# Moving two memsets to VectorE ahead of the input, list-scheduling the last head's chain, and port intervals in the schedule's model

## The chip, the cores and the metric

The kernel runs on one core of a Trainium2 chip. The metric is device time in microseconds (us), the median over several executions. The profile covers one execution and shows its span, which is 1.7 to 2.5 us shorter than the time of the same execution in all runs here (696.9 against 698.68 for the profiled run of the kernel before; 704.4 against 706.56 after). Ratios below are the mean time of one kernel's fast runs over that of the other's of the same rounds, so not quite the ratio of the medians that are quoted. A run counts as fast when its time is within 1.5% of the fastest of the same kernel. Rounds differ: the kernel before has a median of 697.48 to 698.98 in them, so differences between kernels of different rounds are good to about 1.5 us.

Names: PE is TensorE, PEld its weight load, DVE is VectorE, ACT is ScalarE, POOL is GpSimd, SP is SyncE, whose queue issues most transfers. "ps" is PSUM, the matmul output memory; "PV" is the product of the probabilities with V.

## The reference

```python
def reference(A_x, A_wqkv, A_wo, B_x, B_w1, B_b1, B_w2, B_b2):
    x = A_x                                  # 1 x 2048 x 512, bf16
    xn = _layernorm(x)
    # A: softmax attention, 32 heads of 16, over 2048 tokens, then @ wo
    # B: layernorm again, token-mixing MLP 2048 -> 1376 -> 2048 with gelu
    return x + _A_ref(xn, A_wqkv, A_wo) + _B_ref(xn, B_w1, B_b1, B_w2, B_b2)
```

Attention is the bulk: 32 heads x 2048 x 2048 exponentials. The kernel works them off as 1024 tiles of 128 x 1024.

## The kernel before

The kernel is Python code that orders every instruction itself. A model (`Sched`) keeps a time at which each engine comes free; the part up to the end of "block 0" (the first 16 periods of two tiles) is written in fixed order, and the rest comes from a greedy loop that takes at each step what the model says can start first. Each engine's order of instructions is then fixed.

```python
def port_time(self, eng, t):                       # the model's port of VectorE and GpSimd:
    return max(t, self.port_free["pool" if eng == "dve" else "dve"])

def load_lib(lib):                                 # GpSimd's loadable library, with INT64_ADD
    sc.add("pool", lambda e: e.load_library(lib), cost=(LIB_I, LIB_I), name="lib", port=False)

def late_consts():
    load_lib(INT64_LIB)
    sc.add("pool", lambda e: e.memset(wo_t[:], 0.0), ...)
    ...                                            # loads of wo, one small cast (b1col) on GpSimd

# head: layer norm of the first four tiles of x
ln_sums(1); warm_up(N_WARM, 5); ln_stats(0); ...; ln_stats(3)
sc.add("pool", lambda e: e.memset(v17_main[:, :, 16:17], 1.0), ...)   # V's column of ones
for t in range(NPRE):
    ln_norm(t)
late_memsets()                                     # VM, on GpSimd

VM_AT = (2, 8, 12, 15)                             # VM = 13/16 of V, scaled on GpSimd
for period in range(NKT):                          # NKT = 16: block 0
    ...
    block0_work(period)
    if period in VM_AT:
        j = VM_AT.index(period)
        vm_scale(list(range(4 * j, 4 * j + 4)), 0) # a tensor_scalar on GpSimd
    if period == 13:
        ln2_stats()
late_consts()                                      # behind all of it
...                                                # the greedy loop, then tail()
```

An exponential is either one ACTIVATE on ScalarE, or a TENSOR_SCALAR on VectorE with three shifted copies, of which about two go to GpSimd as INT64_ADD. The latter needs four PV products in place of one.

The softmax here doesn't subtract the row's maximum and nothing guards it: scores larger than these inputs give would overflow.

## Time and profile before

| | us |
|---|---|
| time, median of 3 runs | 696.94 (696.93 to 698.19) |
| span of the profiled run | 696.9 |
| first exponential on ScalarE starts | 15.27 |
| last exponential on ScalarE ends | 685.03 |
| first instruction of the last head's chain on VectorE | 688.99 |

A timeline row has start, length, engine, source line, operation, output and input, and in brackets the idle time just ahead with what ended it; "issue" there means that the engine waited for nothing that the profile shows.

### The profile page before, as it was taken

Reading aid. Unit: us, or ns where it says so; the run is one execution under the profiler, and the core shown is the slowest. Engines: PE = TensorE matmul, PEld = TensorE weight load, DVE = VectorE, ACT = ScalarE, POOL = GpSimd, SP = SyncE. Lnnn points to the kernel's source line nnn. Section 1 sums busy time; section 2 is a strip of 40 time slices with the busy share of each in tenths; the row PEclk is TensorE's granted clock in tenths of the full one; section 3 lists DMA queues with packets and bytes.
Section 4 is the critical chain, followed back from the end, with each engine's and each line's share of the span. In section 5 each row is a group of like instructions: output and inputs, shape, how many; then the busy total and the mean of one; then the engine's idle time right before and its main releaser. Section 6 shows DMA issues by size and latency. Waiting matters only on the chain.

```text
span 696.9 us, 29358 instructions
## 1 busy us (share of the span) xinstructions
PE 678.8 (97%) x12916; PEld 312.0 (45%) x12916; DVE 621.3 (89%) x894; ACT 673.2 (97%) x736; POOL 402.2 (58%) x683
## 2 busy tenths in 40 slices
PE   7999999999999999999999999999999999999997
PEld 4433545445544444444444444444444444444443
DVE  7968998998989999989999999898998888888987
ACT  4999999999999999999999999999999999999993
POOL 4544556665356755756666576665766665654642
PEclk9999999999999999999999999999999999999999
DMA  7104200031102200022220212222220222213101
GB/s 211 33 4 82 54 22 20 19 72 28 25 13 52 47 23 19 19 55 46 50 39 22 48 38 54 53 56 53 52 60 20 54 54 57 70 35 81 45 23 44
DMA packets 85728, 32.32 MB, mean 46 GB/s; under 512 B 67424, under 2 KB 85600, under 8 KB 85600
## 3 DMA queue, kind: packets, MB, share of 16 engines
q1 hardware_dynamic: 85168, 30.05, 18.6%
q8 instruction: 101, 1.65, 1.0%
q10 hardware_dynamic: 432, 0.39, 0.2%
q14 instruction: 27, 0.22, 0.1%
HBM read 21.76 MB, written 2.35 MB: 35 GB/s over the span
## 4 chain that ended last, share of the span: by engine, by line
PE 80%; ACT 12%; DVE 4%; DMA 2%; issue 1%; POOL 0%; SPq 0%; DVEq 0%
PE ps L808 32%; PE ps L741 29%; PE ps L839 15%; ACT pT L765 8%; ACT x_sb L765 3%; PE ps L893 2%; DMA denb<-rden_scratch 1%; DVE pT L776 1%; DVE OT L1012 1%; ACT gT_sb L950 1%; DVE hx L549 0%; SPq L431 0%; DMA x_sb<-in_A_x_dram 0%; PE ps L590 0%; DVE oT L1048 0%
## 5 line engine op out<-in xcount | busy, mean ns | idle before, releaser
L765 ACT ACTIVATE pT<-ps 128x1024 bf16<-128x1024 f32 x535 | 523.2, 1132 | 3.3 <-PE ps L741 2.7
L776 DVE TENSOR_SCALAR pT<-ps 128x1024 int16<-128x1024 f32 x221 | 270.1, 1222 | 26.8 <-PE ps L741 20.8
L741 PE MATMUL ps<-QT,KT 32*128 32x512 bf16 x2048 | 284.8, 385 | 5.3 <-ACT pT L765 3.5
L782 POOL INT64_ADD pT<-pT x299 | 181.6, 616 | 129.5 <-DVE pT L785 74.2
L808 PE MATMUL ps<-pT,V 128*32 128x256 bf16 x4716 | 243.8, 276 | 2.9 <-DVE OT L1012 2.5
L765 ACT ACTIVATE x_sb<-ps 128x1024 bf16<-128x1024 f32 x182 | 197.9, 1141 | 0.2 <-PE ps L741 0.2
L741 PEld LDWEIGHTS ps<-QT,KT 32*128 32x128 bf16 x2048 | 78.8, 91 | 183.5 <-ACT pT L765 76.3
L808 PEld LDWEIGHTS ps<-pT,V 128*32 128x32 bf16 x4716 | 107.9, 96 | 85.8 <-issue 66.8
L782 POOL INT64_ADD x_sb<-pT x146 | 89.3, 616 | 57.0 <-DVE pT L785 32.7
L776 DVE TENSOR_SCALAR x_sb<-ps 128x1024 int16<-128x1024 f32 x86 | 105.1, 1222 | 14.7 <-PE ps L741 11.8
L808 PE MATMUL ps<-x_sb,V 128*32 128x256 bf16 x1836 | 116.7, 275 | 1.0 <-DVE OT L1012 0.6
L782 POOL INT64_ADD pT<-x_sb x132 | 79.9, 614 | 48.2 <-DVE pT L785 32.6
L785 DVE TENSOR_SCALAR pT<-pT 128x1024 int16<-128x1024 int16 x154 | 65.1, 426 | 4.5
L808 PE MATMUL ps<-pT,VM 128*32 128x256 bf16 x880 | 61.3, 275 | 0.5 <-DVE pT L785 0.5
L839 PE MATMUL ps<-gT_sb,wblk 128*32 128x512 bf16 (+1 forms) x704 | 61.2, 383 | 0.0
L808 PEld LDWEIGHTS ps<-x_sb,V 128*32 128x32 bf16 x1836 | 46.2, 96 | 31.0 <-issue 23.5
L839 PE MATMUL ps<-hx,wblk 128*32 128x512 bf16 x594 | 52.4, 383 | 0.0
L782 POOL INT64_ADD x_sb<-x_sb x47 | 28.6, 614 | 23.8 <-DVE pT L785 8.0
L847 PE MATMUL ps<-hx,wblk 32*128 32x512 bf16 (+1 forms) x96 | 37.1, 387 | 0.0
L785 DVE TENSOR_SCALAR x_sb<-pT 128x1024 int16<-128x1024 int16 x64 | 27.1, 428 | 1.8
L808 PEld LDWEIGHTS ps<-pT,VM 128*32 128x32 bf16 x880 | 23.3, 96 | 10.6 <-issue 8.8
L785 DVE TENSOR_SCALAR pT<-x_sb 128x1024 int16<-128x1024 int16 x58 | 24.5, 423 | 1.6
(113 smaller groups left out, 460.4 us busy)
## 6 DMA issues: line engine op xcount, KB each, us to landing
wblk<-in_B_w_dram SPq DMA_DIRECT2D x10, 512.0 KB, 4.4
wblk<-in_B_w_dram SPq DMA_DIRECT2D x16, 320.0 KB, 3.6
oC<-OT SPq DMA_DIRECT2D x248, 16.0 KB, 1.8
denb<-rden_scratch SPq DMA_DIRECT2D x124, 32.0 KB, 2.3
xr<-in_A_x_dram SPq DMA_DIRECT2D x16, 128.0 KB, 2.6
dcomp<-OT SPq DMA_DIRECT2D x124, 2.0 KB, 1.7
QT<-Qall SPq DMA_DIRECT2D x120, 16.0 KB, 1.8
out_dram<-osb SPq DMA_DIRECT2D x14, 128.0 KB, 2.0
```

Of the source, the lines that this page charges most:

```text
L741: specs.append(dict(eng="pe", fn=lambda e, r=r, bk=bk: e.matmul(bank(bk), lhsT=KT[32 * r:32 * r + 32, T, 128 * kt:128 * (kt + 1)], rhs=QT[ ...
L765: return [dict(eng="act", fn=lambda e: e.activation(buf(pbuf[n]), ps[:, s_ * 1024:(s_ + 1) * 1024], ACTF.Exp, scale=LN2_128), reads=[("ban ...
L776: return dict(eng="dve", fn=lambda e: e.tensor_scalar(buf_i(w), ps[:, s_ * 1024:(s_ + 1) * 1024], IBIAS, 0.0, ALU.add, ALU.max), reads=[(" ...
L782: return dict(eng=eng, fn=lambda e: e.int64_add(buf_i(o).bitcast(I64), buf_i(w).bitcast(I64), SHIFTS[k] * 0x0001000100010001), reads=[("pT ...
L785: return dict(eng=eng, fn=lambda e: e.tensor_scalar(buf_i(o), buf_i(w), float(SHIFTS[k]), 1.0, ALU.add, ALU.mult), reads=[("pT", w)], writ ...
L808: specs.append(dict(eng="pe", fn=lambda e, c=c, h=h, i=i, off=off: e.matmul(bank(PV_BANK)[32 * c:32 * c + 32, 256 * par:256 * par + 256], ...
L839: specs.append(dict(eng="pe", fn=lambda e, c=c, w=w: e.matmul(bank(EX_BANK)[32 * c:32 * c + w, :], lhsT=lhs_of(32 * c, 32 * c + w), rhs=rh ...
L847: return [dict(eng="pe", fn=lambda e: e.matmul(bank(EX_BANK)[0:dst_rows, :], lhsT=lhs_of(0, dst_rows)[rs], rhs=rhs[rs], start=begin, stop= ...
L893: return [dict(eng="pe", fn=lambda e, ct=ct, c=c: e.matmul(bank(EX_BANK)[32 * c:32 * c + 32, 128 * i:128 * (i + 1)], lhsT=xnT[:, ct, 128 * ...
L950: yield "act", [dict(eng="act", fn=lambda e, ap=ap: e.activation(ap, ap, ACTF.Gelu_apprx_tanh), reads=[("gT", f) for f in fts], writes=[(" ...
L1012: yield "pvev", [dict(eng="dve", fn=lambda e: e.tensor_copy(OT32[:, eb, :], bank(PV_BANK)), reads=[("bank", PV_BANK)], writes=[("OT32", eb)])]
```

## The change

The intent: (1) take V's ones and wo_t's zeros off GpSimd and put them on VectorE, which is idle until x arrives, so that the fourth layer norm no longer waits for GpSimd's memset; (2) let the last head's VectorE chain take its place by readiness, keep VectorE from taking the last two exponentials (D_END), and take the block's o_in transfers out of the way of its denominators; (3) model the shared port as intervals. In passing, the library load and the constants move from behind block 0 to its period 12 (LN2_AT). PER_LIST changes nothing at its value.

```diff
-D_LAST = 31
+PER_LIST = 16
+LN2_AT = 12
+D_END = 1022
...
-    def port_time(self, eng, t):
-        return max(t, self.port_free["pool" if eng == "dve" else "dve"])
+    def port_time(self, eng, t, dur):
+        for a, z in self.port_iv["pool" if eng == "dve" else "dve"]:
+            if t < z and t + dur > a:
+                t = z
+        return t
...
         def late_consts():
             load_lib(INT64_LIB)
-            sc.add("pool", lambda e: e.memset(wo_t[:], 0.0), ...)
...
+        late_memsets()
+        sc.add("dve", lambda e: e.memset(v17_main[:, :, 16:17], 1.0), ...)
+        sc.add("dve", lambda e: e.memset(wo_t[:], 0.0), ...)
         ln_sums(1)
...
+        ln_norm(0)
         ln_stats(3)
-        sc.add("pool", lambda e: e.memset(v17_main[:, :, 16:17], 1.0), ...)
-        for t in range(NPRE):
+        for t in range(1, NPRE):
             ln_norm(t)
-        late_memsets()
...
-            if period == 13:
+            if period == LN2_AT:
                 ln2_stats()
-
-        late_consts()
+                late_consts()
...
+        # task_o_in and task_last: generators for the greedy loop;
+        # the code of task_last stood at the start of tail() before
-                    if n % BN > D_LAST or ...:        # never true
+                    if n >= D_END:
                         continue
```

More of the change, by code (lines that the diff above doesn't have):

```diff
@@ L139, in __init__ @@
         self.pe_log = []
-        self.port_free = {"dve": 0.0, "pool": 0.0}
+        self.port_iv = {"dve": [], "pool": []}
         self.port_op = None
@@ L180, in _time @@
         if port:
-            ready = self.port_time(eng, max(self.free[eng], ready))
+            ready = self.port_time(eng, max(self.free[eng], ready), cost[0])
         if op.is_dma:
@@ L208, in _time @@
         if port:
-            self.port_free[eng] = op.t0 + cost[0]
+            self.port_iv[eng] = self.port_iv[eng][-7:] + [(op.t0, op.t0 + cost[0])]
     def pe_activity(self, t):
@@ L498, in late_consts @@
             load_lib(INT64_LIB)
-            sc.add("pool", lambda e: e.memset(wo_t[:], 0.0), writes=[("wo_t", z) for z in range(4)], cost=(1.75, 1.8))
             for e_ in range(2):
@@ L650, in bass_parallel_sum__softmax_full_mha__mixer_token_mlp__prompt_kernel @@
                writes=[("rcomp", 0)], cost=(1.4, 1.5))
+        late_memsets()
+        sc.add("dve", lambda e: e.memset(v17_main[:, :, 16:17], 1.0), writes=[("Vone",)], cost=(0.6, 0.65))
+        sc.add("dve", lambda e: e.memset(wo_t[:], 0.0), writes=[("wo_t", z) for z in range(4)], cost=(1.1, 1.15))
         ln_sums(1)
@@ L657, in bass_parallel_sum__softmax_full_mha__mixer_token_mlp__prompt_kernel @@
         ln_rstd(1, 2)
+        ln_norm(0)
         ln_stats(3)
-        sc.add("pool", lambda e: e.memset(v17_main[:, :, 16:17], 1.0), writes=[("Vone",)], cost=(2.28, 2.33))
-        for t in range(NPRE):
+        for t in range(1, NPRE):
             ln_norm(t)
-        late_memsets()
         TB = (0, 1, 2, 3)
@@ L705, in block0_work @@
                 warm_up(5, PV_BANK, KT[:, 0, 0:512], [("KTt", 0, z) for z in range(4)])
-            if period >= NKT - 2:
+            if NKT - 2 <= period < PER_LIST:
                 warm_up(3, 4, KT[:, 0, 0:512], [("KTt", 0, z) for z in range(4)])
@@ L1005, in bass_parallel_sum__softmax_full_mha__mixer_token_mlp__prompt_kernel, with task_o_in @@
         ot_free = set()
+        def task_o_in(b):
+            p, e_ = divmod(b, 2)
+            eb, tb_ = b % 2, p % 2
+            yield "gate", lambda: p < 2 or PAIRS[p - 2] in oT_done
+            for c in range(4):
+                h, i = divmod(c, 2)
+                for a in range(2):
+                    ro = 64 * e_ + 32 * a + 16 * i
+                    yield "sp", [dict(dst=oC32[ro:ro + 16, tb_, 256 * h:256 * h + 256],
+                                      src=OT32[32 * c:32 * c + 16, eb, 256 * a:256 * a + 256],
+                                      reads=[("OT32", eb)], writes=[("oC32", tb_, e_, c, a)], name="o_in")]
+            yield "call", lambda: ot_free.add(b)
         def task_epilogue(b):
@@ L1017, in task_epilogue @@
                                   reads=[("OT32", eb)], writes=[("dcomp", eb, c)], name="den_in")]
-            yield "gate", lambda: p < 2 or PAIRS[p - 2] in oT_done
-            for c in range(4):
-                h, i = divmod(c, 2)
-                for a in range(2):
-                    ro = 64 * e_ + 32 * a + 16 * i
-                    yield "sp", [dict(dst=oC32[ro:ro + 16, tb_, 256 * h:256 * h + 256],
-                                      src=OT32[32 * c:32 * c + 16, eb, 256 * a:256 * a + 256],
-                                      reads=[("OT32", eb)], writes=[("oC32", tb_, e_, c, a)], name="o_in")]
-            yield "call", lambda: ot_free.add(b)
+            g_in = dict(gen=task_o_in(b), cur=None)
+            if b == NBLK - 2:
+                yield "call", lambda: (step_gen(g_in), frees.append(g_in))
+            else:
+                yield from task_o_in(b)
             yield "dve", [dict(eng="dve", fn=lambda e: e.reciprocal(rcomp[:, eb, :], dcomp[:, eb, :]),
@@ L1045, in task_epilogue @@
                                              writes=oT_keys(qb, T), cost=(0.2, 0.26))
+            yield "gate", lambda: b in ot_free and (half or b - 1 in ot_free)
             for h in range(2):
@@ L1055, in bass_parallel_sum__softmax_full_mha__mixer_token_mlp__prompt_kernel, with task_last, v, blocks @@
         oT_done = set()
+        t_bf = oT(0).rearrange("p t x -> p (t x)")
+        oL = t_bf[:, 0:512]
+        def task_last():
+            tb_ = 0
+            dk = [("denb", tb_, x, r) for x in range(2) for r in range(4)]
+            def v(ap, half):
+                return ap.rearrange("p (a x) -> p a x", a=2)[:, :, 128 * half:128 * half + 128]
+            def blocks(ap):
+                return ap.rearrange("p (a h b x) -> p a h b x", a=2, h=2, x=32)
+            def op(fn, reads, writes, cost):
+                return "dve", [dict(eng="dve", fn=fn, reads=reads, writes=writes, cost=cost)]
+            yield op(lambda e: e.transpose(denb[:, tb_, :], bank(PV_BANK)), [("bank", PV_BANK)], dk, (0.7, 0.75))
+            rl = rcomp[:, 0, :].rearrange("p (a h b) -> p a h b", a=2, h=2)
+            yield op(lambda e: e.reciprocal(rcomp[:, 0, :], denb[:, tb_, :].rearrange("p (n x) -> p n x", x=32)[:, :, 16]),
+                     dk, [("rcomp", 0)], (0.2, 0.25))
+            ck = [("oC32", tb_, x, c, a) for x in range(2) for c in range(4) for a in range(2)]
+            for half in range(2):
+                yield op(lambda e, half=half: e.transpose(
+                    blocks(oC32[:, tb_, :])[:, :, half], rl[:, :, half, :].unsqueeze(3).to_broadcast([128, 2, 4, 32])),
+                    [("rcomp", 0)], [("rl", half)] + (ck if half == 0 else []), (0.35, 0.4))
+                yield op(lambda e, half=half: e.tensor_tensor(v(oL, half), v(bank(PV_BANK), half), v(oC32[:, tb_, :], half), ALU.mult),
+                         [("bank", PV_BANK), ("rl", half)],
+                         [("oTl", half)] + ([("oTc", 0, z) for z in range(4)] if half == 0 else []), (0.35, 0.4))
         def tail():
@@ L1062, in tail @@
             tbk = [2 * slots[0], 2 * slots[0] + 1, 2 * slots[1], EX_BANK]
-            tb_ = 0
-            dk = [("denb", tb_, x, r) for x in range(2) for r in range(4)]
-            def v(ap, half):
-                return ap.rearrange("p (a x) -> p a x", a=2)[:, :, 128 * half:128 * half + 128]
-            t_bf = oT(0).rearrange("p t x -> p (t x)")
-            oL = t_bf[:, 0:512]
-            osl = [osb[:, 0, :], osb[:, 1, :], t_bf[:, 512:1024], t_bf[:, 1024:1536]]
-            def blocks(ap):
-                return ap.rearrange("p (a h b x) -> p a h b x", a=2, h=2, x=32)
-            sc.add("dve", lambda e: e.transpose(denb[:, tb_, :], bank(PV_BANK)),
-                   reads=[("bank", PV_BANK)], writes=dk, cost=(0.7, 0.75))
-            rl = rcomp[:, 0, :].rearrange("p (a h b) -> p a h b", a=2, h=2)
-            sc.add("dve", lambda e: e.reciprocal(rcomp[:, 0, :], denb[:, tb_, :].rearrange("p (n x) -> p n x", x=32)[:, :, 16]),
-                   reads=dk, writes=[("rcomp", 0)], cost=(0.2, 0.25))
-            ck = [("oC32", tb_, x, c, a) for x in range(2) for c in range(4) for a in range(2)]
-            for half in range(2):
-                sc.add("dve", lambda e, half=half: e.transpose(
-                    blocks(oC32[:, tb_, :])[:, :, half], rl[:, :, half, :].unsqueeze(3).to_broadcast([128, 2, 4, 32])),
-                    reads=[("rcomp", 0)], writes=[("rl", half)] + (ck if half == 0 else []), cost=(0.35, 0.4))
-                sc.add("dve", lambda e, half=half: e.tensor_tensor(v(oL, half), v(bank(PV_BANK), half), v(oC32[:, tb_, :], half), ALU.mult),
-                       reads=[("bank", PV_BANK), ("rl", half)], writes=[("oTl", half)] + [("oTc", 0, z) for z in range(4)] if half == 0 else [("oTl", half)],
-                       cost=(0.35, 0.4))
+            osl = [osb[:, 0, :], osb[:, 1, :], t_bf[:, 512:1024], t_bf[:, 1024:1536]]
             def heads_of(Tm, sti):
@@ L1133, in bass_parallel_sum__softmax_full_mha__mixer_token_mlp__prompt_kernel @@
         for period in range(NKT):
-            for n in (2 * period, 2 * period + 1):
-                for s_ in score_specs(n):
-                    add(s_)
-                sp_ = exp_specs(n)
-                exp_commit(n)
-                add(sp_[0])
-            if period >= 2:
-                for _ in range(2):
-                    pv_emit(0, pv_q[0][0])
+            if period < PER_LIST:
+                for n in (2 * period, 2 * period + 1):
+                    for s_ in score_specs(n):
+                        add(s_)
+                    sp_ = exp_specs(n)
+                    exp_commit(n)
+                    add(sp_[0])
+                if period >= 2:
+                    for _ in range(2):
+                        pv_emit(0, pv_q[0][0])
             block0_work(period)
@@ L1204, in bass_parallel_sum__softmax_full_mha__mixer_token_mlp__prompt_kernel @@
         g_gelu = dict(gen=task_gelu(), cur=None)
-        next_n = BN
+        next_n = 2 * PER_LIST
         ready_q = []
@@ L1257, in est @@
             if s0.get("port"):
-                t = sc.port_time(s0["eng"], t)
+                t = sc.port_time(s0["eng"], t, s0["cost"][0])
             return t
@@ L1367, in bass_parallel_sum__softmax_full_mha__mixer_token_mlp__prompt_kernel @@
                 for qi, n in enumerate(ready_q):
-                    if n % BN > D_LAST or (qi == 0 and len(ready_q) == 1 and False):
+                    if n >= D_END:
                         continue
@@ L1534, in bass_parallel_sum__softmax_full_mha__mixer_token_mlp__prompt_kernel @@
                         pv_block += 1
+                        g = dict(gen=task_last(), cur=None)
+                        step_gen(g)
+                        frees.append(g)
                     else:
```

## The prediction

> **What bounds the kernel now.** I read the page first, then the stretches table, the waits of ScalarE, the chain of waits, and the timelines of the first 60 and last 20 us. The engines' busy shares:
>
> ```profile
> PE 678.8 (97%) x12916; PEld 312.0 (45%) x12916; DVE 621.3 (89%) x894; ACT 673.2 (97%) x736; POOL 402.2 (58%) x683
> ...
> L765 ACT ACTIVATE pT<-ps 128x1024 bf16<-128x1024 f32 x535 | 523.2, 1132 | 3.3 <-PE ps L741 2.7
> ...
> L765 ACT ACTIVATE x_sb<-ps 128x1024 bf16<-128x1024 f32 x182 | 197.9, 1141 | 0.2 <-PE ps L741 0.2
> ```
>
> ScalarE computes 535 + 182 = 717 of the 1024 exponentials; VectorE does the other 307 by integer tricks, with GpSimd's INT64_ADDs. Of ScalarE's exponentials the idle time ahead of them is 3.5 us in all. The stretches table has ScalarE busy 99.64 to 100.00 us of every 100 us between 100 and 600 us, with 110 instructions in 100 us: one exponential each 0.909 us. PE is nearly as full (97.97 to 99.79 of 100). So the time has three pieces: the head until the first exponential (15.27 us), a stream that ScalarE paces (to 685.03 us), and a tail (to 696.9 us). What shortens the head or tail counts in full; what stalls the stream also counts in full, since nothing later has room to catch up.
>
> The head, in the chain of waits:
>
> ```profile
> 7.15 0.63 POOL mv L529
> 7.79 0.03 issue
> 7.81 3.10 DVE hx L549
> 10.92 0.05 issue
> 10.96 0.40 PE ps L577 x4
> ```
>
> and on GpSimd at that time:
>
> ```profile
> 7.73 2.27 POOL L659 MEMSET V<- 128x512 bf16 x1
> ```
>
> The fourth layer norm, some 0.4 us of work, takes 3.10 us on VectorE: it sits behind GpSimd's memset of V's ones (7.73 to 10.00).
>
> GpSimd at the end of block 0, and VectorE beside it:
>
> ```profile
> 42.51 0.65 POOL L618 TENSOR_SCALAR VM<-V 128x544 bf16<-128x544 bf16 x1 [0.73 <-DVE V L573]
> 48.71 1.79 POOL L499 MEMSET wo_t<- 128x2048 bf16 x1 [5.55 <-issue]
> 50.47 0.37 POOL L509 CAST b1col<-b1c_bf 128x11 f32<-128x11 bf16 x1
> 55.43 0.61 POOL L782 INT64_ADD x_sb<-x_sb  x1 [4.60 <-DVE hx L565]
> ```
>
> The 5.55 us that nothing explains are the library load that stands there in the program. The first INT64_ADD comes only at 55.43, after VectorE's 16 second layer norms, and PE had been ordered so as not to need it before 55.8.
>
> The tail:
>
> ```profile
> 681.11 3.92 ACT L765 ACTIVATE pT<-ps 128x1024 bf16<-128x1024 f32 x4
> ...
> 687.20 0.43 DVE L785 TENSOR_SCALAR pT<-pT 128x1024 int16<-128x1024 int16 x1
> 688.19 0.87 DVE L1048 TENSOR_TENSOR wkv_raw<-oC,denb 64x256 bf16<-64x256 f32 x2 [0.57 <-DMA denb<-rden_scratch]
> 688.99 0.70 DVE L1075 STREAM_TRANSPOSE denb<-ps 128x512 f32<-128x512 f32 x1
> ```
>
> ScalarE is through at 685.03, but VectorE has the last exponential (684.56) with its shifts until 687.63, then waits for a transfer of the block before, works it off (0.87), and starts the last chain at 688.99. From there it is 7.9 us to the end.
>
> **What the Trainium skill says.** "SBUF — State Buffer", Who interferes with whom: VectorE in a 2-port mode and GpSimd share a port pair under an exclusive lock, held for the whole instruction; a VectorE instruction with at most one SBUF input outside these modes does not contend. The trace agrees: 3.10 us for the norm. "VectorE: DVE Perf Modes", Zero memsets can be issued as uint32: one cycle per element whatever the type. The trace agrees: 256 elements took 0.27 us. "GPSIMD Engine Reference", 2.1 Instruction dispatch: the first call to a freshly loaded kernel pays about 6 us without a visible instruction. The trace shows 5.55 us. "TensorE: Matmul & The Clock Gate", Part 1: after an idle window of about 3.4 us the PE clock is halved, and needs such a window of work to come back. Before, the granted clock is below 1 only at the start (0.90 over the first 15.3 us).
>
> **The change part by part.**
>
> Head. The two memsets move to VectorE ahead of x. Estimate from the 256 elements: V's 512 elements 0.55 us, wo_t's 1024 uint32 1.08 us; from 1.58 us on this ends at 3.2 us, before x arrives (3.48). GpSimd's VM memsets (1.12 + 0.12 us) move ahead too, from 2.69 to 3.9 us, before its first use at 4.48. Both are hidden. VectorE then: norm 0 goes in before the statistics of tile 3 (0.4 us), so these end at about 7.0; GpSimd adds 0.23 + 0.07 + 0.63 us, to about 8.1; norm 3 ends at 8.6 in place of 10.92. Everything up to the first exponential hangs on it: **-2.3 us**.
>
> Stream. I counted the built instructions: ScalarE has 716 exponentials (717 before), VectorE 308 (307). One fewer at 0.909: **-0.9 us**. The interval model of the port only reorders; I put nothing on it. PER_LIST does nothing at its value. ScalarE would end at 685.03 - 2.3 - 0.9 = 681.8.
>
> Tail. D_END gives the last two exponentials to ScalarE, and the last block's chain may go ahead of the waiting multiplies; o_in is taken out of the way of the denominators. The built order on VectorE ends: exponential, three shifts, transpose, multiply, reciprocal, multiply, transpose and so on. The last shift chain is 1.23 + 3 x 0.4 = 2.4 us and starts some 2 us before ScalarE's end; with the last PV matmuls (0.3) the transpose starts about 0.9 us after ScalarE's end, at 682.7 (before, 3.96 after). The two multiplies (0.87) now lie within the chain: 682.7 + 7.9 + 0.87 = 691.5. Tail net: **-2.2 us**. So far 696.9 - 2.3 - 0.9 - 2.2 = 691.5.
>
> Library. This is the part that the change does not mention. The load of the INT64 library moves from the end of block 0 to period 12, but GpSimd's fourth VM scaling is at period 15. The built instructions show what follows: in front of that scaling stands a reload of the standard library, and behind it another of the INT64 library. Neither is in the kernel's text nor in its schedule's model. Each should cost 5.55 us. GpSimd: second-norm powers end at 41.8 - 2.3 = 39.5; load to 45.05; cast 0.37, 45.4; reload to 51.0; scaling 0.65, 51.6; reload to 57.2; the first INT64_ADD is done at 57.8. The schedule believes GpSimd free before 49: PE's built order has its first wait on GpSimd three scores earlier than before, between matmuls that ran at 51.25 before, so at 51.25 - 2.3 = 48.9. PE is in order, so it stands from 48.9 to 57.8. At most two written score tiles feed ScalarE meanwhile (1.8 us), and the next comes 0.5 us after PE resumes: ScalarE loses 57.8 + 0.5 - 48.9 - 1.8 = 7.6 us: **+7.6 us**. PE's clock falls to half in the stall; 3.4 us of work at half speed put it back up to 1.7 us, of which I take 1.0: **+1.0 us**. Sum: 691.5 + 8.6 = 700.1.
>
> **Rivals.** (a) *The reloads cost little.* For it: a reload also stands ahead of the affine select at the start, and only 0.49 us passes there; but the standard library may have been resident then. If true, 691.5. I give it one in seven. (b) *Reloads cost more.* The kernel's own constant for a load is 7.2 us, against 5.55 in the trace. Two more loads and the moved one at 7.2 give 3 x 1.65 = 5 us more: 705. One in ten. (c) *The head is bound by the loads of x and the weights*, which keep the DMA queues busy to about 15 us: then the 2.3 us shrink. Against it, x's first tiles land at 3.46 and the 256 KB pieces 4.5 us after their issue at about 4, well before they are used at 11.16. It would make 701. (d) *The multiplies in the last chain wait for their transfer.* Before, it landed 15.1 us after the copy that starts it; VectorE's work from that copy to the transpose now adds up to about 14.5 us, and one DMA issue delay of about 1 us goes away but three o_in issues come in. A wait of 0.5 to 2 us is possible: 701 to 702.
>
> **Range and chances.** The centre is 700.0. The stall's length depends on twice a load time measured once, +-2 us; the tail estimate on +-1 us; the stream on +-1 us of scheduling noise. Range 695.5 to 703.5. Over 2% faster means below 683.0, over 2% slower above 710.9: neither follows from any rival; faster 0.01, within 0.96, slower 0.03.
>
> **What would show each step right or wrong.** Right: norm 3 takes about 0.4 us and the first exponential starts at about 13.0; GpSimd shows two idle stretches of over 5 us laid to issue, before the VM scaling and before the first INT64_ADD, which starts near 57; PE has one wait of about 9 us on GpSimd there, ScalarE one of about 7.6 us on PE, and the granted clock drops around 50 to 62 us; ScalarE's last exponential ends near 690, the transpose starts about 0.9 us later, with the multiplies behind it. Wrong: no such wait on GpSimd, and a time near 691; or ScalarE idle in many small pieces in the stream, which would mean the new order itself is worse.

## The result, and the profile after

| | before | after |
|---|---|---|
| time, median of 4 runs each | 697.57 (696.93 to 698.61) | 707.19 (706.56 to 707.45) |
| ratio, 95% interval | 1 | 1.0135 (1.0118 to 1.0153) |
| span of the profiled run | 696.9 | 704.4 |
| first exponential on ScalarE starts | 15.27 | 12.51 |
| last exponential on ScalarE ends | 685.03 | 694.74 |
| last head's chain starts on VectorE | 688.99 | 696.15 |

From the page of the kernel after (busy time and share; then the PE clock granted in each fortieth of the span, in tenths; then two groups with their idle time ahead):

```profile
PE 678.9 (96%) x12918; PEld 310.1 (44%) x12921; DVE 621.9 (88%) x901; ACT 673.6 (96%) x735; POOL 397.7 (56%) x680
...
PEclk9997999999999999999999999999999999999999
...
L771 ACT ACTIVATE pT<-ps 128x1024 bf16<-128x1024 f32 x545 | 530.0, 1129 | 14.4 <-PE ps L747 13.2
...
L771 ACT ACTIVATE x_sb<-ps 128x1024 bf16<-128x1024 f32 x171 | 185.2, 1122 | 0.5 <-PE ps L747 0.2
```

No engine is busy as much as 1 us longer than before. ScalarE's idle time ahead of its exponentials went from 3.5 to 14.9 us, and one slice of the clock reads 7. The timeline of GpSimd shows the cause:

```profile
44.42 0.18 POOL L513 CAST b1col<-b1c_bf 128x11 f32<-128x11 bf16 x1 [5.40 <-issue]
51.49 0.64 POOL L622 TENSOR_SCALAR VM<-V 128x544 bf16<-128x544 bf16 x1 [6.89 <-issue]
57.98 0.60 POOL L788 INT64_ADD x_sb<-x_sb  x1 [5.85 <-issue]
```

Three idle stretches stand where before there was one of 5.55 us, and the listing of the built instructions has a library reload at each:

```
52 L565 TensorTensor mv<-mv,mhalf 128x16
53 L520 ISA                                  reload of library 1 (INT64), the one in the text
54 L513 TensorCopy b1col<-b1c_bf 128x11
55 L622 ISA                                  reload of library 0 (standard)
56 L622 TensorScalarPtr VM<-V 128x4x136
57 L788 ISA                                  reload of library 1
58 L788 ISA x_sb<-x_sb 128x512               the first INT64_ADD
```

On PE and ScalarE, from their timelines:

```profile
48.53 0.39 PE L853 MATMUL ps<-hx,wblk 32*128 32x512 bf16 x1
58.64 0.40 PE L814 MATMUL ps<-x_sb,V 128*32 128x256 bf16 x4 [9.72 <-POOL x_sb L788]
```

```profile
48.95 1.02 ACT L771 ACTIVATE pT<-ps 128x1024 bf16<-128x1024 f32 x1
60.31 1.02 ACT L771 ACTIVATE pT<-ps 128x1024 bf16<-128x1024 f32 x1 [10.33 <-PE ps L747]
62.01 1.02 ACT L771 ACTIVATE pT<-ps 128x1024 bf16<-128x1024 f32 x1 [0.67 <-PE ps L853]
63.57 1.99 ACT L771 ACTIVATE pT<-ps 128x1024 bf16<-128x1024 f32 x2 [0.54 <-PE ps L747]
```

PE stands 9.72 us for the first INT64_ADD, ScalarE 10.33 us for PE, and twice more just after. The stretches table tells why the later gaps exist (columns: us of the stretch, busy us of each engine with instruction counts, then the granted clock, DMA share, GB/s):

```profile
core 0: us, PE busy (x) PEld busy (x) DVE busy (x) ACT busy (x) POOL busy (x), PEclk, DMA share, GB/s
49.00:58.60 9.60, 0.00 (x0) 0.00 (x0) 0.62 (x2) 0.98 (x2) 1.26 (x3) 0.73 0.10 23
58.60:63.50 4.90, 4.86 (x55) 1.47 (x59) 1.65 (x2) 2.05 (x2) 2.37 (x4) 0.50 0.03 7
63.50:75.00 11.50, 11.50 (x230) 5.11 (x230) 10.55 (x15) 11.41 (x13) 6.51 (x11) 0.99 0.02 4
```

For the 4.90 us after the stall PE works at half its clock and leaves ScalarE busy for 2.05 us of it. Finer stretches of the same table put the fall of the clock to half at 53.5 us, 4.6 us after PE's last matmul ahead of the stall, and its return at 63.75, 5.1 us after PE resumed.

The head, by VectorE's timeline and then by the chain of waits:

```profile
3.28 0.48 DVE L656 MEMSET V<- 128x512 bf16 x1 [1.70 <-issue]
3.90 0.91 DVE L657 MEMSET wo_t<- 128x1024 uint32 x1
4.73 0.63 DVE L523 BATCH_NORM_STATS2 stats<-x_sb 128x6 f32<-128x512 bf16 x1
```

```profile
8.05 0.42 DVE hx L553
8.47 0.05 issue
8.52 0.40 PE ps L581 x4
```

The 3.10 us norm is gone from the chain. But VectorE's statistics start at 4.73 us, against 3.48 before, because V's memset comes late.

The tail, on ScalarE and VectorE:

```profile
691.84 2.90 ACT L771 ACTIVATE x_sb<-ps 128x1024 bf16<-128x1024 f32 x3
```

```profile
696.15 0.72 DVE L1089 STREAM_TRANSPOSE denb<-ps 128x512 f32<-128x512 f32 x1 [1.04 <-PE ps L814]
696.79 0.37 DVE L1064 TENSOR_TENSOR wkv_raw<-oC,denb 64x256 bf16<-64x256 f32 x1
```

The chain starts 1.41 us after ScalarE's last exponential (3.96 before) and needs 8.25 us to the end (7.91 before, without the multiply shown here).

So the span splits as follows: head -2.76 (15.27 to 12.51), stream from first to last exponential +12.47 (669.76 to 682.23), tail -2.21 (11.87 to 9.66): 696.9 - 2.76 + 12.47 - 2.21 = 704.4.

### The profile page after: what moved, and what is told of

Read it like the earlier page. It is cut to its first block, busy times and chain, and to the rows that moved or that the text cites. A ratio compares the mean times of both kernels' runs of the same rounds, so it can differ in the third digit from the quotient of the medians.

```text
span 704.4 us, 29372 instructions
## 1 busy us (share of the span) xinstructions
PE 678.9 (96%) x12918; PEld 310.1 (44%) x12921; DVE 621.9 (88%) x901; ACT 673.6 (96%) x735; POOL 397.7 (56%) x680
## 4 chain that ended last, share of the span: by engine, by line
ACT 66%; PE 27%; DVE 3%; issue 2%; DMA 1%; POOL 0%; DVEq 0%; POOLq 0%
ACT pT L771 50%; ACT x_sb L771 16%; PE ps L814 10%; PE ps L747 10%; PE ps L845 4%; DVE pT L782 1%; ACT gT_sb L956 1%; DMA denb<-rden_scratch 1%; PE ps L899 1%; PE ps L650 0%; PE ps L581 0%; DVE OT L1031 0%; PE ps L594 0%; PE ps L1121 0%; DVE oT L1064 0%
## 5 line engine op out<-in xcount | busy, mean ns | idle before, releaser
L771 ACT ACTIVATE pT<-ps 128x1024 bf16<-128x1024 f32 x545 | 530.0, 1129 | 14.4 <-PE ps L747 13.2
L782 DVE TENSOR_SCALAR pT<-ps 128x1024 int16<-128x1024 f32 x224 | 273.9, 1223 | 38.4 <-PE ps L747 32.1
L788 POOL INT64_ADD pT<-pT x309 | 187.1, 614 | 135.8 <-DVE pT L791 84.7
L814 PE MATMUL ps<-pT,V 128*32 128x256 bf16 x4768 | 248.6, 276 | 2.0 <-DVE OT L1031 1.7
L771 ACT ACTIVATE x_sb<-ps 128x1024 bf16<-128x1024 f32 x171 | 185.2, 1122 | 0.5 <-PE ps L747 0.2
L782 DVE TENSOR_SCALAR x_sb<-ps 128x1024 int16<-128x1024 f32 x84 | 102.7, 1223 | 10.0 <-PE ps L747 8.0
L788 POOL INT64_ADD pT<-x_sb x117 | 71.3, 617 | 48.9 <-DVE pT L791 30.4
L791 DVE TENSOR_SCALAR pT<-pT 128x1024 int16<-128x1024 int16 x146 | 61.6, 425 | 4.3
L791 DVE TENSOR_SCALAR x_sb<-pT 128x1024 int16<-128x1024 int16 x70 | 30.2, 431 | 2.1
L814 PE MATMUL ps<-x_sb,VM 128*32 128x256 bf16 x396 | 28.1, 273 | 0.0
```

Source lines behind the costliest of these rows:

```text
L771: return [dict(eng="act", fn=lambda e: e.activation(buf(pbuf[n]), ps[:, s_ * 1024:(s_ + 1) * 1024], ACTF.Exp, scale=LN2_128), reads=[("ban ...
L782: return dict(eng="dve", fn=lambda e: e.tensor_scalar(buf_i(w), ps[:, s_ * 1024:(s_ + 1) * 1024], IBIAS, 0.0, ALU.add, ALU.max), reads=[(" ...
L788: return dict(eng=eng, fn=lambda e: e.int64_add(buf_i(o).bitcast(I64), buf_i(w).bitcast(I64), SHIFTS[k] * 0x0001000100010001), reads=[("pT ...
L791: return dict(eng=eng, fn=lambda e: e.tensor_scalar(buf_i(o), buf_i(w), float(SHIFTS[k]), 1.0, ALU.add, ALU.mult), reads=[("pT", w)], writ ...
L814: specs.append(dict(eng="pe", fn=lambda e, c=c, h=h, i=i, off=off: e.matmul(bank(PV_BANK)[32 * c:32 * c + 32, 256 * par:256 * par + 256], ...
```

## The experiments

Theory: the two reloads that appear in the built program, and nothing else, cost more than the rest of the change gains. Rivals: the reordered stream is worse in itself, and the gap is only where it shows; VectorE's norms, moved ahead of its first exponential, hold the stream; the head takes back what it gains. Eleven kernels ran, all with correct results.

### The fourth scaling on VectorE (e1_scale_on_vector)

```diff
-                vm_scale(list(range(4 * j, 4 * j + 4)), 0)
+                vm_scale(list(range(4 * j, 4 * j + 4)), 0, "dve" if j == 3 else "pool")
```

> The changed kernel with one edit: the fourth VM scaling of block 0 goes to VectorE, so that no GpSimd instruction of the standard library stands behind the early load of the INT64 library. The built order then has no reload. Theory (the two hidden reloads hold PE, and with it ScalarE): the 10.3 us gap of ScalarE near 50 us and the low clock behind it are gone, and the time falls by about 12 us from the changed kernel's 707.2, to about 695, which is 0.3% to 0.5% below the kernel before. Rival A (the new order from the interval model of the port is worse in itself, the gap only shows it): the time stays above 702. Rival B (VectorE's second norms ahead of the first exponential hold the stream): a ScalarE gap of several us stays near 45 to 55 us.

Measured: 693.8 us (692.9 to 694.71), before 698.98 in these rounds, ratio 0.9931 (0.9915 to 0.9948). GpSimd's timeline:

```profile
44.58 0.18 POOL L513 CAST b1col<-b1c_bf 128x11 f32<-128x11 bf16 x1 [5.57 <-issue]
45.44 0.61 POOL L788 INT64_ADD x_sb<-x_sb  x1 [0.68 <-DVE x_sb L782]
```

One load instead of three, the first INT64_ADD 12.5 us earlier, and ScalarE's longest wait in the stream is 0.5 us. Against the changed kernel's median (of other rounds) this is 13.4 us. Both rivals fall: the order is just as new, and VectorE's 16 norms stand ahead of its first exponential here too (4.29 us from 39.91 on, the exponential at 44.12).

### The load behind block 0 again (e2_load_late)

```diff
                 ln2_stats()
-                late_consts()
+
+        late_consts()
```

> The changed kernel with the load of the INT64 library, and what stands with it, put back behind period 15, behind the fourth VM scaling, as in the kernel before; the second-norm statistics stay at period 12. No reload is built. Theory: as with the scaling on VectorE, about 695 to 696; GpSimd's one load ends about 46 us, so at most a small wait on GpSimd (under 1 us) could be left. Rival A: above 702. If this one is 2 us or more slower than the scaling on VectorE, the early load is worth something by itself.

Measured: 691.73 us (691.47 to 692.69), ratio 0.9906 (0.9890 to 0.9923) in the same rounds. It is better than expected and 2.1 us better than e1, so no worth of the early load shows; the two also differ in the engine of the fourth scaling, so this does not measure the load's place by itself. Part of the difference is known: 715 exponentials on ScalarE against 716, and two of e1's four runs had a lower granted clock (0.998) and spans of 692.7 and 692.9, against 691.1 and 691.3 at full clock. What costs e1's two runs that clock was not looked into.

### One GpSimd instruction back behind the load (e3_one_op_back)

```diff
-            sc.add("pool", lambda e: e.tensor_copy(b1col[:], b1c_bf[:]), ...)
+            sc.add("pool", lambda e: e.tensor_scalar(b1col[:], b1c_bf[:], 1.0, None, ALU.mult), ...)
```

This is an edit to e1. The orders of the other four engines are identical to e1's; GpSimd has this one instruction changed and two reloads more.

> The kernel with the fourth scaling on VectorE, and in it only the 128x11 cast of b1 on GpSimd, which stands behind the library load, written as a tensor_scalar times 1. The built order of every other engine is the same; on GpSimd two reloads come in around this one instruction. Theory: the whole loss of the changed kernel comes back: a GpSimd idle of some 5.5 plus 6.9 plus 5.9 us, a ScalarE gap of about 10 us, time 11 to 13 us above the kernel with the scaling on VectorE (about 707). Rival A (order, not reloads): within 1 us of it.

Measured: 705.98 us (705.32 to 706.33), ratio 1.0105 (1.0090 to 1.0120); 12.2 us above e1. GpSimd's timeline and the waits of ScalarE (us in total, times, longest):

```profile
51.70 0.30 POOL L513 TENSOR_SCALAR b1col<-b1c_bf 128x11 f32<-128x11 bf16 x1 [12.69 <-issue]
57.85 0.60 POOL L788 INT64_ADD x_sb<-x_sb  x1 [5.84 <-issue]
```

```profile
ACT x_sb L771 <- PE ps L747: 11.8, 3, 11.4
```

This settles the cause. An instruction on eleven elements per partition brings back nearly the whole loss (12.2 of 13.4 us), because two loads (12.69 us) stand ahead of it and one (5.84 us) behind it.

### The head alone (e4_head_alone)

The kernel before with only the head's lines of the diff above (the two memsets, late_memsets and ln_norm(0)).

> The kernel before with only the head of the change: the memsets of V's ones and wo_t on VectorE ahead of x, VM's memsets ahead on GpSimd, norm 0 ahead of the statistics of tile 3. Theory: the first exponential comes at 12.5 us as in the changed kernel (15.27 before), and the time falls by 2.7 us, to about 694.9; wo_t's memset (1.8 us on GpSimd near 49 us) being gone may add up to 1 us. Rival (the stream takes the gain back because it is paced by something fixed in time, such as the loads): less than 1 us faster.

Measured: 694.53 us (694.25 to 695.18), ratio 0.9943 (0.9928 to 0.9958): 4.5 us below the 698.98 of these rounds. The first exponential starts at 12.51. That is more than the 2.76 us of the head. Part of it is the state of the comparison: six of the seven runs of the kernel before in these rounds have the lower clock (0.997 or 0.998) that e7 below is about, and the one at full clock took 697.5, only 3.0 us more than e4. The rest was not taken apart. The greedy loop, started differently, also ended differently: VectorE's last shifts were done by 681.3, 1.2 us ahead of ScalarE's last exponential, where before they ran 2.6 us past it. What VectorE waited for then was a transfer of the block before:

```profile
683.60 0.87 DVE L1049 TENSOR_TENSOR wkv_raw<-oC,denb 64x256 bf16<-64x256 f32 x2 [1.93 <-DMA denb<-rden_scratch]
```

This wait did not set the end by itself: in the chain of waits PE works on 76 PV matmuls (2.07 us) until 684.40, and VectorE's transpose starts at 684.46, as soon as both are done.

### The port model (e8_old_port_model)

e2 with `port_time` and its bookkeeping as before. The built program is, instruction for instruction, that of the head and tail parts put into the kernel before; so moving the statistics to period 12 does nothing.

> The changed kernel with the load put back late and the port as before in the schedule's model (one time at which it comes free, not intervals). The built program is the same, instruction for instruction, as the kernel before with the head and the tail of the change alone. ScalarE then has 718 exponentials, against 715 with the intervals. Theory (ScalarE paces the stream): 3 x 0.909 = 2.7 us slower than the 691.7 with the intervals, about 694.4, so that the tail adds nearly nothing to the head alone (694.5). Rival (the tail is worth its 2.2 us, the intervals nothing): about 692.

Measured: 694.86 us (694.74 to 694.88), ratio 0.9959 (0.9945 to 0.9974), 3.1 us above e2's median; e6 below, an edit of e2 without effect on the time, has 691.8 in the same rounds as e8 and confirms it. So the intervals, to which I gave nothing, are a real gain. ScalarE has 718 exponentials here and 715 in e2, and 3 x 0.909 = 2.7 us would be most of it. ScalarE's last exponentials, in e8 and then in e2, show less:

```profile
680.85 2.00 ACT L768 ACTIVATE pT<-ps 128x1024 bf16<-128x1024 f32 x2
```

```profile
675.40 5.76 ACT L771 ACTIVATE pT<-ps 128x1024 bf16<-128x1024 f32 x6
```

From the first exponential (12.50 in both) to the end of the last it is 670.35 us in e8 and 668.66 in e2, so 1.7 us lie in the stream; 1.1 us lie in the tail (9.65 against 8.54), and 0.6 us of the difference between the two profiled runs lie outside the span. The three exponentials are thus shown as part of the gain, not as all of it.

And on this schedule the tail part adds nothing to the head alone (694.86 against 694.53): the wait for the transfer is gone, but PE still had 78 PV matmuls to do (2.21 us in the chain of waits) before the chain could start, as it had 76 in e4.

### The limit at the end (e11_no_end_limit)

```diff
-D_END = 1022
+D_END = 1 << 20
```

An edit to e9 (below), so that VectorE may take the last exponentials as before.

> The kernel with the ones behind the head, and without D_END's limit, so that VectorE may take the last exponentials, as in the kernel before. The built program has 714 exponentials on ScalarE against 715. Theory: ScalarE ends 0.9 us earlier, but VectorE's shifts end later, so the time is within 1 us of the one with the limit; if the limit is worth what I gave it in the prediction, it is 2 us slower.

Measured: 692.18 us (691.88 to 692.37) against e9's 690.16 in the same rounds. The limit is worth 2.0 us there. ScalarE is through earlier (its last exponential ends at 679.03 against 680.41), yet VectorE's shifts end at 681.6 and the last chain starts at 682.01 against 680.81. The expectation of "within 1 us" was wrong; the alternative that it names, 2 us, held. With e8 this says that the tail part's worth depends on how the schedule happens to end.

### The late memset: three runs (e5, e6, e10)

e5 swaps the two memsets on VectorE, e6 puts VM's memsets on GpSimd behind the head, e10 splits V's ones; all are edits to e2.

```diff
 # e5
-  memset V's ones; memset wo_t
+  memset wo_t; memset V's ones
 # e6
-  late_memsets()            # ahead of the head
+  late_memsets()            # after ln_norm(NPRE)
 # e10
-  e.memset(v17_main[:, :, 16:17], 1.0)
+  for z in range(2): e.memset(v17_main[:, 256 * z:256 * z + 256, 16:17], 1.0)
```

> The changed kernel with the load put back late, and the two memsets that moved to VectorE in the other order (wo_t, written as uint32, first; V's ones, strided bf16, second). In the changed kernel the first of them stood 1.70 us and began at 3.28. If something of V's memset itself waits (the port, while GpSimd's memsets run until 3.6), then wo_t's begins at about 1.6 and ends at 2.5, and V's begins late. If VectorE had no instruction to run (issue), then wo_t's memset also begins at about 3.3.

> The changed kernel with the load put back late, and VM's memsets on GpSimd behind the head instead of ahead of it. If V's memset on VectorE waits for GpSimd's VM memsets, it begins at about 2.7 or earlier, VectorE's statistics begin at 3.5 to 4.1 instead of 4.73, the first exponential comes 0.6 to 1.2 us earlier than 12.51, and the time falls by as much from 691.7. If it is issue, V's memset begins at 3.28 again and nothing changes (within 0.3 us).

> The changed kernel with the load put back late, and V's ones on VectorE in two memsets of 256 elements. In every run so far this memset is shown with 0.48 us and 1.70 us of idle, charged to issue, just ahead of it, whatever stood ahead and whatever GpSimd did. If the 1.70 us belongs to its elements (the strided 2-byte writes), each half shows about 0.85 us ahead and the sum stays 2.2 us. If it is a fixed cost of such an instruction, each half shows 1.7 us and the sum is 3.9 us. If it is a fixed cost of the first one alone, the second shows none.

Measured: 691.7 (one run), 691.8 (691.58 to 692.06; ratio 0.9916, 0.9900 to 0.9933) and 691.66 us (one run): no time is in it. VectorE's timeline in e5, then in e10:

```profile
1.74 0.91 DVE L656 MEMSET wo_t<- 128x1024 uint32 x1 [0.16 <-issue]
4.35 0.48 DVE L657 MEMSET V<- 128x512 bf16 x1 [1.70 <-issue]
```

```profile
2.40 0.27 DVE L657 MEMSET V<- 128x256 bf16 x1 [0.82 <-issue]
3.62 0.27 DVE L657 MEMSET V<- 128x256 bf16 x1 [0.94 <-DVE V L657]
```

In e5 the wo_t memset starts at once and V's still has 1.70 us ahead of it, although GpSimd runs nothing from 3.6 to 5.4 us. In e6, with nothing on GpSimd from 2.7 us on, V's memset again starts at 3.28. So it is not the port. In e10 the idle time halves with the elements (0.82 and 0.94). So I put it down to the writing of these elements: 1.70 + 0.48 = 2.18 us for 512 two-byte elements in steps of 17, or 4.3 ns each (2.30 us in the two halves of e10), of which the profile then shows as busy only the last part. GpSimd's memset of the same elements took 2.27 us. VectorE was no quicker. Why such writes are slow was not tested.

### PE kept busy in the head of the kernel before (e7_before_gap_filled)

```diff
-N_MID = (1, 1, 1, 2)
+N_MID = (1, 1, 12, 2)
```

> The kernel before with 12 warm-up matmuls instead of one behind the third transposes, which fill PE's idle stretch from 8.5 to 10.9 us while the fourth norm waits. The norm is as late as before. Theory (the head gained more than the norm's 1.55 us because PE no longer idles and keeps its full clock): the first exponential comes at about 14.0 instead of 15.27, though nothing that it waits for is earlier. Rival (the chain behind the norm was shortened by the order of the instructions): it stays at 15.2 or later.

A stretch of the kernel before (columns as in the stretches table above), and ScalarE's first exponentials in e7:

```profile
13.00:15.00 2.00, 2.00 (x20) 1.54 (x18) 0.35 (x2) 0.47 (x1) 0.03 (x1) 0.50 0.76 120
```

```profile
13.92 3.77 ACT L765 ACTIVATE pT<-ps 128x1024 bf16<-128x1024 f32 x4 [0.49 <-PE ps L741]
```

In the profiled run of the kernel before, PE idled 2.51 us for the late norm and then worked at half clock from 13 to 15 us (by finer stretches from 12.2 to 15.6). In e7 the clock is 1.00, and the first exponential comes 1.35 us earlier (13.92). x arrived 0.12 us earlier in this run too; the other 1.2 us go with the clock: from the end of the fourth norm to the first exponential it is 4.36 us in the kernel before, and 3.14 us both in e7 and in the changed kernel. The one time is 697.65 us (before: 697.19 to 699.16), which shows no gain, and the spans say why: of the kernel before's 7 runs in these rounds, five have a clock of 1.0 and spans of 695.4 to 695.9, two a clock of 0.997 or 0.998 and spans of 697.2 and 697.3. e7's 695.8 lies among the first. So the kernel before very likely runs the head either way by chance (only the profiled run's trace shows where its clock was low), and the profiled run was one of the worse. One run of e7 cannot tell whether filling the gap kept the clock up, or chance did.

### The best of it (e9_ones_behind_head)

e2 with the memset of V's ones back on GpSimd, after ln_norm(NPRE); wo_t's zeros stay on VectorE.

```diff
-        sc.add("dve", lambda e: e.memset(v17_main[:, :, 16:17], 1.0), ...)
...
         ln_norm(NPRE)
+        sc.add("pool", lambda e: e.memset(v17_main[:, :, 16:17], 1.0), ...)
```

> The changed kernel with the load put back late, and the memset of V's ones back on GpSimd, behind the head (after the statistics of the fifth tile), where no layer norm of the head follows it; wo_t's stays on VectorE ahead of x. Theory: VectorE's statistics begin with x at 3.4 to 3.5 instead of 4.73, the first exponential comes 1.2 us earlier than 12.51, near 11.3, and the time is about 690.5. Rival: the memset on GpSimd (2.3 us from about 10.3 on) holds copies of VectorE in the head by the port, and the gain is under 0.5 us.

Measured: 690.16 us (690.12 to 690.73), ratio 0.9884 (0.9866 to 0.9903) to the kernel before (698.65 in these rounds). VectorE's statistics, GpSimd's memset and the first exponentials:

```profile
3.52 0.69 DVE L523 BATCH_NORM_STATS2 stats<-x_sb 128x6 f32<-128x512 bf16 x1 [0.87 <-DMA x_sb<-in_A_x_dram]
```

```profile
10.52 2.27 POOL L693 MEMSET V<- 128x512 bf16 x1
```

```profile
11.47 3.77 ACT L771 ACTIVATE pT<-ps 128x1024 bf16<-128x1024 f32 x4 [0.49 <-PE ps L747]
```

The statistics start with x again, and the first exponential comes 1.03 us earlier than in e2; the time falls by 1.6 us. This version is below both kernels: 8.5 us below the kernel before's median of its own rounds, and 17 us below the changed kernel's 707.19.

## Why the prediction was right or wrong

It named what happened and in which place, but was 7.2 us short (700.0, range to 703.5, measured 707.19). The step that failed is the size of the stall: "+7.6 us" for the library and "+1.0 us" for the clock, 8.6 us together, measured as 10.33 + 0.67 + 0.54 = 11.5 us of idle ScalarE. Two more things were missing from the sum: 2.2 us between span and time, and 1.8 us lost elsewhere in the stream. By its own steps:

- **Head, -2.3 us.** Measured -2.76, for partly other reasons. The step "V's 512 elements 0.55 us ... both are hidden" failed: they took 2.18 us (e5, e6, e10) and put the statistics off by 1.25 us. Norm 3 ended at 9.37, not 8.6. So the norm gave 1.54 us (10.91 to 9.37), not 2.3. The other 1.22 us lie between the norm and the first exponential and go with the clock: in the profiled run of the kernel before PE was at 0.50 from 13 to 15 us, and after it was not (e7). The prediction quotes that low clock (0.90 over the head) and gives it no part in the head's gain; that the sum came close is luck.
- **Stream, -0.9 us for one exponential, and nothing for the interval model.** The count was right, the nothing was not. With the reloads gone (e2 against e8) the intervals give three exponentials and 3.1 us. Besides the stall, ScalarE lost in the changed kernel a further 1.8 us over the stream, a remainder and not something that I measured by itself; I had allowed 1 us either way. The largest piece in the trace is a wait of 0.88 us for PE, just before 313.37 us; the cause of the whole stays open.
- **Tail, -2.2 us.** Measured -2.21 in the trace, with two errors that cancel: the transpose started 1.41 us after ScalarE's end, not 0.9, since the last PV matmuls held it for 1.04 us and not 0.3; and the chain with its multiplies took 8.25 us, not 7.9 + 0.87. The transfer did not hold the multiplies (rival d falls). e11 shows 2.0 us for the limit alone, and e8 shows none for the whole part on another schedule.
- **Library, +7.6 us.** The mechanism was right (e1, e3), the size was not: ScalarE's gap was 10.33 us, of which about 9.2 us belong here and the rest to the clock. The stall began where I had put it (48.9; measured 48.92). Each reload was put at 5.55 us; the standard library's took 6.89 and the INT64 library's second one 5.85, less 0.8 us saved ahead of them, so PE resumed at 58.64 instead of 57.8. "At most two written score tiles" fed ScalarE only until 49.97, not 50.7. The first made the gap 0.8 us longer, the second 0.7 us.
- **Clock, +1.0 us.** Half speed lasted 5.1 us after PE resumed. I had ScalarE resume 0.5 us after PE; it took 1.67 us, and gaps of 0.67 and 0.54 us followed: 1.17 + 0.67 + 0.54 = 2.4 us. No run separates the clock from the stall, so that all of this is the clock's is argued.
- **Span and time.** I started the sum from the span of a run that took 698.68 us (696.9) and called the result a time. By the 2.2 us between the two in the changed kernel the prediction was short before any step of it. That 696.9 lies near the kernel before's median time (697.57) is chance: the profiled run was 1.1 us slower than the median.

These add up: the stall's end 0.8, ScalarE's earlier stop 0.7, clock 1.4, rest of the stream 1.8, head -0.46, span to time 2.2, and 0.6 between the profiled run and the median, are 7.0 of the 7.2 us (700.0 is rounded down from the sum of 700.1). Of the rivals, (a) falls (e1, e3), (b) names the right direction but not the size, and (c) falls: x's loads did not bind, since e9 brings the first exponential to 11.47 us.

## What to carry to other kernels

Read the built instructions, not only the source: what a builder inserts, here two library reloads of 5.9 and 6.9 us set off by one instruction on the wrong side of a load, is in no diff and in no model of the schedule. Where every engine's order is fixed and two engines are full, such a stall on a third engine that is only 56% busy can be lost in full: here PE stood 9.72 us, and the one instruction of e3 cost 12.2 us. When a change bundles parts, measure them apart: here the head, the intervals and the end's limit each were gains of 2 to 4.5 us on the schedule they were tried on (the head's 4.5 against runs of the kernel before with a slow head), hidden behind one loss of 12 us.

## What the Trainium skill lacked or had wrong

- "GPSIMD Engine Reference", 2.1 Instruction dispatch, puts the first call after a load at about 6 us. The runs agree roughly (5.40 to 5.85 us for the INT64 library, 6.89 us ahead of the first instruction of the standard one, 12.69 us for two loads in a row). No page was found that says that a tensor_scalar on GpSimd behind a load of another library brings two reloads into the built program, while a tensor_copy there brings none (e1 and e3: 12.2 us apart).
- "VectorE: DVE Perf Modes", Zero memsets can be issued as uint32, says one cycle per element whatever the type. 1024 contiguous uint32 took 1.07 us with the 0.16 us of idle ahead of them (e5, e9), which fits the 0.27 us of 256; 512 two-byte elements in steps of 17 took 2.18 us, 4.3 ns each, of which 1.70 us appear as idle (e5, e6, e10). That section speaks of types and not of steps between elements; what the skill says of steps elsewhere was not tested here.
- "TensorE: Matmul & The Clock Gate", Part 1, speaks of an idle window of about 3.4 us before the clock drops, and such a window of work to bring it back. It also says that the window is free-running, which fits a head that is slow in some runs only. Here the clock fell after 2.51 us of idle and 1.26 us of work (to 0.50 from 12.2 to 15.6 us, in the profiled run of the kernel before); in the stall it fell 4.6 us after PE's last matmul and came back after 5.1 us of work.
